# A gated linear attention followed by a mixer: three more transposes on the transfer queue, one product folded into another, and a new order

## The chip, the cores and the metric

The kernel runs on one core of a Trainium2 chip. The metric is the device time of one execution in microseconds (us), the lower the better. A core has five engines that each work through their own instruction list in order: PE (TensorE, matrix products; its weight loads are listed apart as PEld), DVE (VectorE), ACT (ScalarE), POOL (GpSimd) and SP (SyncE, which here issues every transfer). The transfers themselves run on 16 DMA engines. Products land in PSUM, in eight banks; everything else is worked on in SBUF.

## The reference

For 4 batches, 8 heads, 768 time steps and a head width of 48, a recurrent state is decayed, updated and read at each step; the result, as a 768 x 384 matrix `x` for each batch, goes through a low-rank mix over time and an MLP over the 384 columns.

```python
for t in range(S):
    state = alpha[:, :, t, :, None] * state + einsum('bhd,bhe->bhde', k[:, :, t], v[:, :, t])
    y[:, :, t] = einsum('bhd,bhde->bhe', q[:, :, t], state)
x = y.transpose(0, 2, 1, 3).reshape(B, S, H * D)
h = x.transpose(0, 2, 1) @ U @ V                 # U 768 x 32, V 32 x 768
u = x + h.transpose(0, 2, 1)
out = u + maximum(u @ w_ch1, 0) @ w_ch2          # 384 -> 1536 -> 384
```

## The kernel before

Each batch's 768 steps are cut into six chunks of 128 (`c` from 0 to 5). `b0` to `b3` below are the four batches, so the third batch is `b2`. A chunk loads four tiles of 192 KB (alpha, k, q, v) into the 40 `io` buffers. The chunks named by `PAIRS` (all of b0, four of b1) go through `stage_pair`, the others through `stage_gla`. `stage_gla` does this for a chunk:

- ACT takes the logarithm of alpha (`lt`, line 549); PE sums it over time (lines 556 and 558); ACT takes the exponentials `ai` and `aa` (566, 567).
- POOL or DVE multiplies k by `ai` and q by `aa` into one tile, `rkq` (577).
- k and q are transposed into `kqt`. In b2 and in the last two chunks of b1 PE does that: two groups of four 128 x 128 products (line 591) into two PSUM banks, and two copies out of PSUM (lines 290 on DVE, 288 on ACT, through the helper `copy`). In b3, by the tuple `QUEUE_T`, one `dma_start_transpose` on SP's queue does it (line 603), which reads and writes SBUF alone.
- PE forms the scores from `kqt` (619), DVE masks them into `pm` (629), PE forms the state's update from `rkq` and `rv` (642, not from `kqt`), DVE and POOL carry the state on (669, 653), and PE forms the chunk's output (681, 686), which ACT or DVE copies into `xb` (288, 290).

`stage_mix` forms the low-rank mix of a batch, `mlp1` the first MLP product (line 815, 24 groups of three products a batch, with a ReLU on ACT at 825 or on DVE at 827) and `mlp2` the second (line 841, 18 groups of four a batch, 21 in b3, with an addition on DVE at 847 and a store on SP at 850 or 852). In b1 to b3 the mix adds the V product to `xb` and stores `u` in `ub` (732, 742). In b0, by `SUM_U`, `u` transposed is summed in PSUM (752, 764) for `mlp1`, and `u` itself is formed besides: one V product for each chunk (line 755) into a bank of its own, and a DVE addition into `ub` (765), which `mlp2` adds to its product at 847. In b3 `u` is transposed by three transfers on SP's queue (770).

Nothing schedules at run time. `TABLE` lists all steps in one order with the engine that each goes to, and `SLOTS` the buffer each takes; every engine runs its own steps in that order and waits on semaphores for what they need. SP is one queue too: a transfer that waits for its operand holds back every transfer behind it. There are four `rkq` and four `kqt` buffers, and a transposing transfer waits until the last reader of its `kqt` buffer is through.

Of the kernel before, what the change touches and what calls it, by code (L numbers as in the profile page):

```python
# [11 lines left out]
ALU = mybir.AluOpType  # L12
# [17 lines left out]
F+DB+SJXPK2ALHAJhPJYDK1AK6GB9SJlPIyDKNAJTPKOAJmDK5GKgABySI-PK4AJiDKPAK3AJLPLiAKKGKQDBuSJPPJADJDPJQABxSJRPJUAKhAJBPLfABzS  # L30
JbPJCDKiALhAI3PKjAJEDLxAKlGCMSJVPJcAJMDJfPI4DJWAB3SKRGKZPKSPJgDLJPI7PKaDKkGLKAB6SJSDI9PLNALgAI8DK8PLjGCFSK7PK+AI+DJHPKeG
LMAK9DKmPCESOEAJjPLkDJIAKtPKnPLLACVSKuDI5PKoAKTPKvGJkAJNPB5SKVDKpAJZPI6DKzGKUAJdPB7SJaDJOAK-PJeAKqPKWPKrDLlPGHPCCSKXDLCP
GIPLADB-SLnDJFPLBDLzPCBSJ-PJGAKYDNhAJJPLIGLDDCGSNjPLPGKsDJtPNkACUSNlALEDKAPLOGL1ANoDNmAKbPCQSL0AKBPJKDL3GLdAKcDLQPNnALXP
CDSLFPLSAL2GLYDLmPLRPCLSLoALZDL5PJuPNpGLTAL7DKCDLsPKwPLGDGJPCYSKxALtDL4PCXSGKDJvPOWAL6DOYPLyGJwDCISLUPOZALuGL8PLWDLpPOoA
CKSJ5PObAL+DJnPL9DNqSOqPLrDJ6POsALVDJoPGeSLqDNyACWSLaPOrAJ7PCZSOcAOaAL-POuALbALvPCSSMADOtAJpPLwAJ8DN0PJqDMBPCHSNrPMCAN3A
MDPNsDCRSOwGJzPMEDKEPMGDOvGCNSMHDJ0PMFDNzGOxSMIPJ1PMKDNiAMLDMNPMMDO6ACJSKFPMJDN1AOdGCOSNtDMOANuPMRPJ2DMPPOeGN4AN2AKGPMQD
NwPMSDOfSO8PMZPO+AMlPMaDMXPCPSN6DMmAMVPO9ACTSN5DNxAM7PNvDMYAN-PN7SM5PMWDOADNBPM8DOGPKDSKHDOHAOgPOFGM9POpAGGSNCDM6AOLGMtP
OhDGYSOJAOIAM-PCaSM+AOBGMfPOMDGdSNAAM3PMgDOXGONSORPMTPOSDM1POiDMUAMrPCbSOKAM4DOTGMxPMsAM2DMnPMuAMyDPAGOjPMpPMoAOkDOmPO-G
N8POnDOyPMzPN9DPBSO7GMhPN+DMdPOzDGLSMjPO0DO1PJ9SMbPMkAOlDGMSMqAMvPMiAO2DNDPMcAMwAO3DO4PMeAPCPO5DOOPNcPPDDOPDNEPOQDOCPNFP
PEDOUPODDPFPOVDNIPPGANGDM0APHPNSPPIAPJPNdPPKDPNDNTPPLDPMDPOPNUPPRDPTSPPDNJPPSDPQDNePNVDPUSNNPNXPPVSNOPNYPKISNKPJySNZPNWS  # L40
NPPPYPPWPPZDPaPPXDPyPNLDPbAP6PNQDNMSPePP7ANRSPwPPfDJrSP0PGXSP8PP1APqPPkPPrDQCPPlAPuPPzAQDDPgPNaDP+PPvDPhAP4PPxAP9APmPP5D
PsPP-DPiPNfDPcPPtDNgSQEPPjDPdAJ3SQfPF-SQAPJ+SP2PQBDGFSQQPPnDP3AJsSQkPJ4SPoPNHSQRPGSSPpDQGPQFDNbSGRSQlPJxSQHPQLPQmPQMPQnD
QIPQoSQSPGASQJDQNPQTDQKSQgPQODQUSQVPQPSQhPQWPQiDQaPQXPQjSQbPQYDQcPQZSQdDQeS
"""
SLOTS = """
ABCDEFAGAHAIAAJBBCKCALADBMENBAOFBPBCGBCHAQCAACEGRAHDSCTAEBBFGUAABDDVCHAWFECDABBXCDAYCBGCECZFBCCCaAAEDbFDGcACEABBAdAGBACF
HDBCACCeEHECDfBBBACgGEhBBAHADiCBCCGEjDBFCkHBAlmBGDAEAnDAHFBAACAGCAADBACAHDDFFBGECBCHAHAGICDEFCBKAGCECADHBBALFHJBBMADOAGB
CBBAEFQAPDNDGSBCHFBRDGACUCBTAEBVCDWHADBBAECGHBDAZBFEBHAAGXDFAHYAEBBaDAbdCeHfgFGDDCFGEDBhEGCFiAEcCCDljkFnBAmEADCBBBCFAEDC
CDFFCAADBGEBCGHEACBDBACKHBAABJBBHCAAICEQDABAPCDAABNBFOECHAACLBACFDREADDGSCABFAVBECDDHUDBBGWADFECHABGTCFBZBCAXBBDEAaCBHBM
BBCADFYACCCEAbDDBCFdCEAeACfAEghAFAcjBDCDCACGEBkHBBDCAAAAmCBCCEABiBGGFJCAACEBHDCDBFCCIBDEHDBDHBQADKCDBPEBHAAGAFAENCBBEAGA  # L50
FBABHDOCEBEFAAGBDCCWBHACCEFACHLDEFCDBBAHCGEFAADDACHCGCEAHDBDCGEABCBDGEUCBBDGHFACDFGASHFCGBDBRCZGDEHCGECGTBEFGCXDHEBAGCDB
AabYMFjDm
"""


# [98 lines left out]
def mm(*cols):  # L154
    return sum(max(c / 2.4 + 2.5, 25.0) for c in cols)
# [3 lines left out]
def kernel(  # L159
# [178 lines left out]
    def paired(b, c):  # L338
        return c // 2 < PAIRS[b]
# [22 lines left out]
    def xk(b, xb, c):  # L362
        return [(xb, c, 0), (xb, c, 1)] if paired(b, c) else [(xb, c)]
# [331 lines left out]
    def stage_mix(b, xb, ub, uT):  # L695
# [63 lines left out]
                    P.add({"PE": mm(TW)}, lambda e, j=j, f=f_h: f(e, j), r=[utx, ("ve", tt)], w=[tb[j]])  # L759
                    P.add({"ACT": 390, "DVE": 470}, lambda e, j=j, tt=tt, tb=tb: copy(e, uT()[:, j, tt * TW : (tt + 1) * TW], tb[j]()[:, 0:TW]), r=[tb[j]], w=[(uT, tt, j)])  # L760
        for c in range(NC):
            hb = Buf(bank) if b in SUM_U else None
            if b in SUM_U:
                P.add({"PE": mm(DM)}, lambda e, c=c, hb=hb: nc.tensor.matmul(hb()[:, 0:DM], lhsT=(ve_sb if paired(b, c) else vm_sb)[:, c * C : (c + 1) * C], rhs=utx(), start=True, stop=True), r=[utx, ("ve" if paired(b, c) else "vm", c // NT)], w=[hb])
                P.add({"DVE": 465}, lambda e, c=c, hb=hb: nc.vector.tensor_tensor(ub()[:, c, :], xb()[:, c, :], hb()[:, 0:DM], op=ALU.add), r=[hb] + xk(b, xb, c), w=[(ub, c)])
            if b in QUEUE_U:
                if c % 2 == 1:
                    P.add(
# [7 lines left out]
            elif c % 2 == 1 and b not in SUM_U:  # L776
                ub2 = Buf(bank)

                def f_tr(e, c=c, ub2=ub2):
                    t = bf(ub2()).rearrange("p (e c) -> p e c", c=C)  # L780
                    n = 0
                    for cc in (c - 1, c):
                        for j in range(NCT):
                            nc.tensor.matmul(t[:, n, :], lhsT=ub()[:, cc, j * C : (j + 1) * C], rhs=ident, start=True, stop=True, is_transpose=True)  # L784
                            n += 1

                P.add({"PE": mm(*[C] * 6)}, f_tr, r=quarters(ub, (c - 1, c)), w=[ub2])
# [6 lines left out]
                P.add({"DVE": 450, "ACT": 710}, f_ev, r=[ub2], w=[(uT, c // 2)])  # L794

    def u_half(uT, ct, tt, by_chunk):
        if not by_chunk:
# [30 lines left out]

            P.add({"ACT": 395, "DVE": 470}, g, r=[hb], w=[(h1, tt, jt)])

    def mlp2(b, ub, h1, c):
        tt = c // NT
        ou = Buf(io)
        parts = [(0, DM)] if (b, c) != (B - 1, LAST) else [(0, CUT), (CUT, DM)]
        for n, (lo, hi) in enumerate(parts):
            hb = Buf(bank)
            for g in range(3):

                def f(e, g=g, hb=hb, lo=lo, hi=hi):
                    for jt in range(4 * g, 4 * g + 4):  # L840
                        nc.tensor.matmul(  # L841
                            hb()[:, 0 : hi - lo], lhsT=h1()[:, jt, c * C : (c + 1) * C], rhs=w2_sb[:, jt, lo:hi],
                            start=(jt == 0), stop=(jt == NJ - 1),
                        )

                P.add({"PE": mm(*[hi - lo] * 4)}, f, r=[(h1, tt, jt) for jt in range(4 * g, 4 * g + 4)] + [("w2", jt) for jt in range(4 * g, 4 * g + 4)], w=[hb])
            P.add({"DVE": 468}, lambda e, hb=hb, lo=lo, hi=hi: nc.vector.tensor_tensor(flat(ou)[:, lo:hi], ub()[:, c, lo:hi], hb()[:, 0 : hi - lo], op=ALU.add), r=[hb] + ([(ub, c)] if b in SUM_U else quarters(ub, (c,))), w=[(ou, n)])  # L847
# [11 lines left out]
    for b in range(B):  # L859
# [3 lines left out]
        for c in range(NC):  # L863
# [3 lines left out]
            else:  # L867
                x = stage_gla(b, c, whole, xb)
                whole = [(x, 0, x)]
        stage_mix(b, xb, ub, uT)  # L870
        mlp1(b, uT, h1, 0)
        mlp1(b, uT, h1, 1)
        for c in range(NC):
            mlp2(b, ub, h1, c)
    P.run("".join(TABLE.split()), "".join(SLOTS.split()))


# [28 lines left out]
```

## Time and profile before

| | us |
|---|---|
| runs shown: median (lowest to highest of 3) | 160.37 (159.43 to 160.62) |
| the profiled execution | 159.65 |
| its span, first to last instruction | 157.9 |

The span leaves 1.75 us around it. In the page of the profile a busy share is the time in which an engine had an instruction in it. PE's products are pipelined, so that share says when PE had nothing, not how fast it ran; the granted clock is 1.00 throughout. The chain of waits goes back from the last instruction and names at each step what released it. In the timeline a row gives start, duration, engine, line, output and inputs, and a count of like instructions.

### The profile page before, as it was taken

The page shows a single profiled execution, that of the slowest core. Times are in us where ns is not written, and L with a number is a line of the kernel's source. Part 1 is how long each engine was busy: PE and PEld are TensorE (multiplying, and loading weights), DVE is VectorE, ACT ScalarE, POOL GpSimd, SP SyncE. Part 2 cuts the span into 40 slices and gives each one's busy share as a digit, 9 for nine tenths or more (in the row PEclk, how much of TensorE's full clock was granted, in tenths as well). Part 3 has the DMA queues.
Part 4 walks back from the last instruction along what each step waited for, and adds up shares of the span by engine and source line. Part 5 has one row for each costly group of instructions (what it writes and reads, how often), then busy time and mean ns, then how long its engine had stood idle before and what let it go on. Part 6 is the DMA issues. An engine that isn't in the chain of part 4 may idle for free.

```text
span 157.9 us, 4730 instructions
## 1 busy us (share of the span) xinstructions
PE 147.7 (94%) x1836; PEld 98.7 (63%) x1836; DVE 118.6 (75%) x264; ACT 83.6 (53%) x219; POOL 58.6 (37%) x93
## 2 busy tenths in 40 slices
PE   0499999999999999999999999999999999999992
PEld 0268777766665665767668676766667556665662
DVE  5048998999899788869799978989999714484252
ACT  3667899775866823988838464457362001441000
POOL 8336787387838300446358223416610000000000
PEclk9999999999999999999999999999999999999999
DMA  5999999999999999999799998996860073406662
GB/s 130 280 312 309 257 263 253 337 317 274 279 254 236 269 177 200 201 216 209 156 210 222 179 200 176 201 153 152 174 143 3 15 142 124 150 34 159 185 224 100
DMA packets 96966, 31.08 MB, mean 197 GB/s; under 512 B 90640, under 2 KB 96912, under 8 KB 96944
## 3 DMA queue, kind: packets, MB, share of 16 engines
q1 hardware_dynamic: 96944, 30.78, 82.0%
q8 instruction: 14, 0.23, 0.6%
q14 instruction: 8, 0.07, 0.1%
HBM read 23.89 MB, written 4.72 MB: 181 GB/s over the span
## 4 chain that ended last, share of the span: by engine, by line
PE 72%; SPq 14%; DMA 5%; DVE 3%; issue 2%; ACT 1%
PE ps L815 29%; PE ps L841 28%; SPq L347 11%; DMA io<-in_alpha_dram 5%; PE ps L619 2%; PE ps L686 1%; PE ps L556 1%; PE ps L591 1%; PE ps L784 1%; PE ps L681 1%; DVE rkq L577 1%; SPq L295 1%; SPq L320 1%; PE ps L642 1%; PE ps L732 1%
## 5 line engine op out<-in xcount | busy, mean ns | idle before, releaser
L841 PE MATMUL ps<-w_sb,h1t 128*128 128x384 bf16 (+2 forms) x300 | 52.8, 320 | 0.0
L815 PE MATMUL ps<-uT,w_sb 128*128 128x384 bf16 x288 | 52.0, 326 | 0.0
L825 ACT ACTIVATE h1t<-ps 128x384 bf16<-128x384 f32 x50 | 23.1, 499 | 28.8 <-PE ps L815 28.7
L815 PEld LDWEIGHTS <-w_sb 128*128 128x128 bf16 x288 | 26.6, 98 | 16.0
L841 PEld LDWEIGHTS <-h1t 128*128 128x128 bf16 x300 | 26.8, 97 | 15.0
L827 DVE TENSOR_SCALAR h1t<-ps 128x384 bf16<-128x384 f32 x46 | 24.1, 552 | 12.9 <-PE ps L815 12.2
L629 DVE TENSOR_TENSOR pm<-ps,maskc 128x512 bf16<-128x512 f32 x28 | 17.7, 681 | 1.8 <-PE ps L619 1.3
L847 DVE TENSOR_TENSOR io<-ub,ps 128x384 f32<-128x384 bf16 (+2 forms) x25 | 13.1, 532 | 6.1 <-PE ps L841 5.8
L577 POOL TENSOR_TENSOR rkq<-io,aa 128x384 bf16<-128x384 f32 x9 | 8.2, 915 | 19.6 <-PE ps L815 10.3
L461 DVE TENSOR_TENSOR pm<-ps,maskp 128x512 bf16<-128x512 f32 x20 | 13.3, 686 | 1.6 <-PE ps L450 1.2
L292 POOL CAST rv<-io 128x384 bf16<-128x384 f32 x17 | 9.5, 557 | 11.6 <-DMA io<-in_v_dram 6.7
L577 POOL TENSOR_TENSOR rkq<-io,ai 128x384 bf16<-128x384 f32 x11 | 10.0, 916 | 6.0 <-DMA io<-in_k_dram 4.7
L288 ACT CAST xb<-ps 128x192 bf16<-128x192 f32 (+1 forms) x20 | 7.2, 374 | 9.0 <-PE ps L686 7.0
L742 DVE TENSOR_TENSOR ub<-xb,ps 128x288 bf16<-128x288 bf16 x24 | 9.3, 449 | 2.7 <-PE ps L732 2.5
L290 DVE COPY kqt<-ps 128x512 bf16<-128x512 bf16 x21 | 8.7, 418 | 2.3 <-PE ps L426 1.8
L292 POOL CAST w_sb<-io 128x384 bf16<-128x384 f32 x14 | 8.2, 587 | 4.1 <-DMA io<-in_moe_w_ch_dram 4.0
L288 ACT COPY kqt<-ps 128x512 bf16<-128x512 bf16 x15 | 8.7, 597 | 1.7 <-PE ps L426 0.7
L566 ACT ACTIVATE ai<-ps 128x384 bf16<-128x384 f32 x14 | 6.9, 495 | 3.5 <-PE ps L558 2.9
L549 ACT ACTIVATE lt<-io 128x384 bf16<-128x384 f32 x14 | 7.1, 524 | 2.8 <-issue 2.8
L567 ACT ACTIVATE aa<-ps 128x384 bf16<-128x384 f32 x14 | 6.8, 495 | 3.3 <-PE ps L558 1.7
L408 POOL TENSOR_TENSOR rkq<-io,aa 128x384 bf16<-128x384 f32 x8 | 7.2, 910 | 3.4 <-ACT aa L401 3.2
L426 PE MATMUL ps<-ident,rkq 128*128 128x128 bf16 x80 | 8.3, 236 | 0.1
(117 smaller groups left out, 222.8 us busy)
## 6 DMA issues: line engine op xcount, KB each, us to landing
io<-in_alpha_dram SPq DMA_DIRECT2D x24, 192.0 KB, 3.8
io<-in_v_dram SPq DMA_DIRECT2D x24, 192.0 KB, 3.9
io<-in_k_dram SPq DMA_DIRECT2D x24, 192.0 KB, 4.1
io<-in_q_dram SPq DMA_DIRECT2D x24, 192.0 KB, 3.8
io<-in_moe_w_ch_dram SPq DMA_DIRECT2D x24, 192.0 KB, 4.2
out_dram<-io SPq DMA_DIRECT2D x13, 192.0 KB, 1.9
out_dram<-io SPq DMA_DIRECT2D x20, 96.0 KB, 2.2
out_dram<-io SPq DMA_DIRECT2D x1, 120.0 KB, 1.7
```

The costliest lines, as they stand in the source:

```text
L288: nc.scalar.copy(dst, src)
L292: nc.gpsimd.tensor_copy(dst, src)
L347: lambda e: nc.sync.dma_start(t().rearrange("p (h j) d -> p h (j d)", j=2), src[b, hs, sl, :].rearrange("h (p j) d -> p h (j d)", j=2)),
L461: nc.vector.tensor_tensor(dst, s2, maskp.to_broadcast([C, 2, 2, C]), op=ALU.mult)
L577: eng.tensor_tensor(dst()[:, :, 0:D], a(), x(), op=ALU.mult)
L629: nc.vector.tensor_tensor(pm()[:, :, par, :], s2, maskc.to_broadcast([C, HP, C]), op=ALU.mult)
L742: nc.vector.tensor_tensor(v(ub), v(xb), qb[g]()[:, 0 : NT * W].rearrange("p (c d) -> p c d", c=NT), op=ALU.add)
L815: nc.tensor.matmul(hb()[:, 0:TW], lhsT=w1_sb[:, ct, jt * 128 : (jt + 1) * 128], rhs=u_half(uT, ct, tt, b in QUEUE_U), start=(ct == 0), sto ...
L825: nc.scalar.activation(dst, hb()[:, 0:TW], AF.Relu)
L827: nc.vector.tensor_scalar_max(dst, hb()[:, 0:TW], 0.0)
L841: nc.tensor.matmul(hb()[:, 0 : hi - lo], lhsT=h1()[:, jt, c * C : (c + 1) * C], rhs=w2_sb[:, jt, lo:hi], start=(jt == 0), stop=(jt == NJ - 1),
L847: P.add({"DVE": 468}, lambda e, hb=hb, lo=lo, hi=hi: nc.vector.tensor_tensor(flat(ou)[:, lo:hi], ub()[:, c, lo:hi], hb()[:, 0 : hi - lo], ...
```

## The change

1. `QUEUE_T` also holds chunks 3, 4 and 5 of b2. Their k and q are transposed by three transfers on SP's queue in place of 24 PE products and six copies out of PSUM.
2. b0's V product is the first product of the `mlp2` group in its own PSUM bank, with `start` set there and no longer on the first of the twelve. The six additions into `ub` (765) are gone, b0 uses no `ub`, and the addition at 847 takes `xb` in place of `ub`. The number of products stays the same. `utx` and `xb` of b0 are held until its `mlp2` is through.
3. `TABLE` and `SLOTS` are new: every engine's order, which engine does a step that two could do, and the buffers. The table is one line shorter, so line numbers of the changed kernel are lower by one up to `stage_mix`.

```diff
 TABLE = """
-BASA8SBDSABSBISBESA9SCcAA+SCePA-SC0GBJSAFGCfAChABQSDjAAJPCzABBSDlPCgABCSCiDC1PDnABKSCjDCkPBYSCdGCmABMSAGPDmABGSC4AC3AClP
+BESDKAA+SBASCzAA8SCcACePC1PBISDMPDjABBSCfACgACjGA-SC4AA9SBDSBCSC2AC5DBJSCdGC3AC6GBKSDlPDoAC0GC7PChAC9ADmAClPCnACiDCkPCmA
...
-    QUEUE_T = tuple((3, c) for c in range(6))
+    QUEUE_T = tuple((3, c) for c in range(6)) + ((2, 3), (2, 4), (2, 5))
...
         for c in range(NC):
-            hb = Buf(bank) if b in SUM_U else None
-            if b in SUM_U:
-                P.add({"PE": mm(DM)}, lambda e, c=c, hb=hb: nc.tensor.matmul(hb()[:, 0:DM], lhsT=(ve_sb if paired(b, c) else vm_sb)[:, c * C : (c + 1) * C], rhs=utx(), start=True, stop=True), r=[utx, ("ve" if paired(b, c) else "vm", c // NT)], w=[hb])
-                P.add({"DVE": 465}, lambda e, c=c, hb=hb: nc.vector.tensor_tensor(ub()[:, c, :], xb()[:, c, :], hb()[:, 0:DM], op=ALU.add), r=[hb] + xk(b, xb, c), w=[(ub, c)])
...
-    def mlp2(b, ub, h1, c):
+    def mlp2(b, xb, utx, ub, h1, c):
+        low = b in SUM_U
...
                 def f(e, g=g, hb=hb, lo=lo, hi=hi):
+                    if low and g == 0:
+                        nc.tensor.matmul(hb()[:, lo:hi], lhsT=ve_sb[:, c * C : (c + 1) * C], rhs=utx()[:, lo:hi], start=True, stop=False)
                     for jt in range(4 * g, 4 * g + 4):
                         nc.tensor.matmul(
                             hb()[:, 0 : hi - lo], lhsT=h1()[:, jt, c * C : (c + 1) * C], rhs=w2_sb[:, jt, lo:hi],
-                            start=(jt == 0), stop=(jt == NJ - 1),
+                            start=(jt == 0 and not low), stop=(jt == NJ - 1),
                         )
...
-            P.add({"DVE": 468}, lambda e, hb=hb, lo=lo, hi=hi: nc.vector.tensor_tensor(flat(ou)[:, lo:hi], ub()[:, c, lo:hi], hb()[:, 0 : hi - lo], op=ALU.add), r=[hb] + ([(ub, c)] if b in SUM_U else quarters(ub, (c,))), w=[(ou, n)])
+            P.add({"DVE": 468}, lambda e, hb=hb, lo=lo, hi=hi: nc.vector.tensor_tensor(flat(ou)[:, lo:hi], (xb if low else ub)()[:, c, lo:hi], hb()[:, 0 : hi - lo], op=ALU.add), r=[hb] + (xk(b, xb, c) if low else quarters(ub, (c,))), w=[(ou, n)])
```

The order moves at three places on SP that the prediction speaks of. First the start of the queue, which feeds b0. Before, the first rows are:

```order
L347 DMA io0_134<-in_alpha_dram 128x4x96
L347 DMA io1_135<-in_alpha_dram 128x4x96
L347 DMA io2_136<-in_v_dram 128x4x96
L296 DMA v_in_65<-in_moe_V_dram 32x768
L347 DMA io3_137<-in_alpha_dram 128x4x96
L347 DMA io4_138<-in_alpha_dram 128x4x96
L347 DMA io5_139<-in_k_dram 128x4x96
```

Now they are:

```order
L346 DMA io0_134<-in_alpha_dram 128x4x96
L346 DMA io1_135<-in_q_dram 128x4x96
L346 DMA io2_136<-in_alpha_dram 128x4x96
L346 DMA io3_137<-in_alpha_dram 128x4x96
L346 DMA io4_138<-in_alpha_dram 128x4x96
L346 DMA io5_139<-in_k_dram 128x4x96
L346 DMA io6_140<-in_v_dram 128x4x96
```

The alpha of b0's chunk 0, with which PE begins in both orders, was the second transfer and is the fourth; the load of V (`v_in`) has gone back to the 28th place. The last of b0's 24 loads was the 28th transfer and is the 26th.

Second, the place where the three new transposes stand, among the loads of b2 and b3. Before, the same stretch of the queue holds loads alone:

```order
L354 DMA io23_157<-in_k_dram 128x8x48
L354 DMA io26_160<-in_q_dram 128x8x48
L354 DMA io12_146<-in_alpha_dram 128x8x48
L354 DMA io24_158<-in_alpha_dram 128x8x48
L354 DMA io27_161<-in_v_dram 128x8x48
L354 DMA io29_163<-in_v_dram 128x8x48
```

Now it holds (`kqt1`, `kqt2` and `kqt3` are those of b2's chunks 3, 4 and 5):

```order
L353 DMA io26_160<-in_q_dram 128x8x48
L602 DMA_TRANSPOSE kqt1_190<-rkq0_80 128x8x128
L353 DMA io25_159<-in_v_dram 128x8x48
L353 DMA io28_162<-in_alpha_dram 128x8x48
L602 DMA_TRANSPOSE kqt2_191<-rkq3_83 128x8x128
L602 DMA_TRANSPOSE kqt3_192<-rkq2_82 128x8x128
L353 DMA io19_153<-in_v_dram 128x8x48
```

Behind the first of them 21 loads of b2 and b3 are still queued.

Third, the end of the transposes, with the last loads of b3. Before:

```order
L603 DMA_TRANSPOSE kqt1_190<-rkq2_82 128x8x128
L852 DMA out_0_dram<-io30_164 128x384
L850 DMA out_0_dram<-io37_171 64x384
L850 DMA out_0_dram<-io0_134 64x384
L354 DMA io22_156<-in_q_dram 128x8x48
L850 DMA out_0_dram<-io39_173 64x384
L603 DMA_TRANSPOSE kqt2_191<-rkq0_80 128x8x128
L354 DMA io11_145<-in_v_dram 128x8x48
L603 DMA_TRANSPOSE kqt0_189<-rkq2_82 128x8x128
```

Now (`kqt0` is that of b3's chunk 5, the last `kqt1` that of its chunk 4):

```order
L602 DMA_TRANSPOSE kqt2_191<-rkq3_83 128x8x128
L353 DMA io16_150<-in_k_dram 128x8x48
L353 DMA io7_141<-in_v_dram 128x8x48
L353 DMA io22_156<-in_v_dram 128x8x48
L849 DMA out_0_dram<-io5_139 64x384
L602 DMA_TRANSPOSE kqt0_189<-rkq2_82 128x8x128
L602 DMA_TRANSPOSE kqt1_190<-rkq1_81 128x8x128
```

Ahead of the last transpose stood, since the first load of b2, 48 loads, five transposes and five stores (four of 96 KB and one of 192 KB); now 48 loads, eight transposes and one store of 96 KB stand there.

More of the change, by code (lines that the diff above doesn't have):

```diff
@@ L53 @@
+BFCCBCHAECHBAABACIBDABCDBJKNPACCABCOBBDGFLBHEADGEQAADFGDRBCBHSCEAFGDABADCBBHFDBDMWVEBCGAACEFABACBXEYAABCCGCBUaBFHDZABGBE
+bcHAAFGBCHCBCDABAGAFdCATBfelDCCCBCDBHCEDFAHDkjABCCDDnEABAACAAHCDFBEBCHDFCBCmHEDDBCGPBGCBCHBOANDAEKCFBCBDCHSBEDEBFBCCBHEB
+AAGDBCBALCHGDAEHDGBCFDCCEBQHGBHFWACBEBADCADGHCABABCDGDRHDCBGBAFHDCBDAFAHAYUVFBBDEGHFEXDHMEBHGACHFACHFGEDFADBZcTlEjHf
 """
@@ L794, in stage_mix @@
                 P.add({"DVE": 450, "ACT": 710}, f_ev, r=[ub2], w=[(uT, c // 2)])
+        return utx
     def u_half(uT, ct, tt, by_chunk):
@@ L842, in f @@
                             hb()[:, 0 : hi - lo], lhsT=h1()[:, jt, c * C : (c + 1) * C], rhs=w2_sb[:, jt, lo:hi],
[L843 removed]
+                            start=(jt == 0 and not low), stop=(jt == NJ - 1),
                         )
[L846 to L847 removed]
+                P.add({"PE": mm(*[hi - lo] * 4)}, f, r=[(h1, tt, jt) for jt in range(4 * g, 4 * g + 4)] + [("w2", jt) for jt in range(4 * g, 4 * g + 4)] + ([utx, ("ve", tt)] if low and g == 0 else []), w=[hb])
+            P.add({"DVE": 468}, lambda e, hb=hb, lo=lo, hi=hi: nc.vector.tensor_tensor(flat(ou)[:, lo:hi], (xb if low else ub)()[:, c, lo:hi], hb()[:, 0 : hi - lo], op=ALU.add), r=[hb] + (xk(b, xb, c) if low else quarters(ub, (c,))), w=[(ou, n)])
             if paired(b, c):
@@ L869 @@
                 whole = [(x, 0, x)]
-        stage_mix(b, xb, ub, uT)
+        utx = stage_mix(b, xb, ub, uT)
         mlp1(b, uT, h1, 0)
@@ L873 @@
         for c in range(NC):
-            mlp2(b, ub, h1, c)
+            mlp2(b, xb, utx, ub, h1, c)
     P.run("".join(TABLE.split()), "".join(SLOTS.split()))
```

62 lines of the change are left out of this document (29 added, 33 removed).

## The prediction

> **What bounds the kernel now.** I read the page's busy shares and slices first, then a table of busy time by stages, then the chain of waits.
>
> ```profile
> span 157.9 us, 4730 instructions
> PE 147.7 (94%) x1836; PEld 98.7 (63%) x1836; DVE 118.6 (75%) x264; ACT 83.6 (53%) x219; POOL 58.6 (37%) x93
> DMA  5999999999999999999799998996860073406662
> ```
>
> PE leads, but a busy share averages over unlike stages; the transfers are near full for three quarters of the span. The table, with columns window, length, busy time (and count) of each engine, granted clock, share of the DMA engines and GB/s, separates them:
>
> ```profile
> 14.30:31.40 17.10, 16.44 (x355) 12.68 (x354) 15.84 (x36) 15.38 (x46) 10.28 (x16) 1.00 1.02 279
> 31.40:55.00 23.60, 23.45 (x319) 14.86 (x318) 21.45 (x48) 16.94 (x45) 15.33 (x26) 1.00 1.03 273
> 55.00:88.00 33.00, 33.00 (x391) 22.38 (x390) 28.25 (x59) 21.72 (x58) 13.38 (x18) 1.00 1.00 197
> 88.00:117.00 29.00, 28.79 (x347) 19.18 (x346) 25.86 (x53) 15.38 (x42) 10.96 (x14) 1.00 0.90 174
> 117.00:124.90 7.90, 7.90 (x143) 5.10 (x140) 6.40 (x13) 1.97 (x6) 0.00 (x0) 1.00 0.12 30
> 124.90:155.00 30.10, 30.10 (x204) 18.73 (x196) 14.23 (x29) 4.58 (x10) 0.00 (x0) 1.00 0.47 136
> ```
>
> Until 31.4 the recurrence of b0 runs while loads arrive, and DVE (15.84 of 17.10), ACT and the transfers are all nearly full. From 31.4 to 155 PE is without work for only 0.15 + 0.21 us in the rows shown. From 55 to 88 the DMA share is 1.00 as well.
>
> ```profile
> PE 72%; SPq 14%; DMA 5%; DVE 3%; issue 2%; ACT 1%
> 31.57 1.00 PE ps L815 x6
> 71.95 0.22 PE ps L591 x4
> 131.57 10.24 PE ps L815 x63
> 145.22 9.79 PE ps L841 x72
> 155.03 0.30 DVE io L847
> ```
>
> The chain (start, duration, what) goes through SP's loads, then PE from the first MLP product at 31.57 to 155. So a microsecond of PE work removed after 31 shortens the span by one, as long as PE's next operand is there. The transfers could undo that.
>
> **The change part by part.** The sum is made against the profiled execution, 159.65 us (span 157.9 and 1.75 around it); that is 0.72 below the median 160.37 of the runs shown, so the result is carried over to the median.
>
> *Transposes on PE.* Six groups of four leave. A group takes 0.22 us on the chain (above), so 6 x 0.22 = 1.3 us. All six lie in the stages 55 to 88 and 88 to 117, where PE had no gap to swallow them: -1.3 us on the path.
>
> ```profile
> L290 DVE COPY kqt<-ps 128x512 bf16<-128x512 bf16 x21 | 8.7, 418 | 2.3 <-PE ps L426 1.8 <-PE ps L591 0.4
> L288 ACT COPY kqt<-ps 128x512 bf16<-128x512 bf16 x15 | 8.7, 597 | 1.7 <-PE ps L426 0.7 <-PE ps L591 0.5 <-DVE pm L461 0.3
> L765 DVE TENSOR_TENSOR ub<-xb,ps x6: 545/545/555, 29.0 to 34.5; 128x384 bf16<-128x384 bf16 x6
> ```
>
> *Copies and additions.* By the order DVE does five copies fewer and ACT one: 5 x 0.418 = 2.1 and 0.6 us; the six additions are 6 x 0.545 = 3.3 us of DVE. Both run beside PE. PE's idle time of 0.36 us after 31.4 is all that they can give back there, so I count 0, with -0.4 as the far end. If that cover were absent, DVE being the bound, they would give 5.4.
>
> *The V product.* Six products stay, in another bank: 0 on PE. The new wait, the first group of four for `utx`, ends long before: `utx` serves the first MLP product at 31.57, and the first group of four comes after some 17 us more of PE work in the new order, counted at the durations of the rows. Holding `xb` and `utx` of b0 costs nothing as long as b0's last group is done (after 52 us of PE work) before b2 needs that `utx` (after 80).
>
> *SP and the DMA engines.* Three transposes come in.
>
> ```profile
> L603 SPq DMA_TRANSPOSE kqt<-rkq x6: 1232/1412/2187, 88.4 to 113.9; - x6
> DMA to landing us min/median/max: 3.1/3.4/3.5
> 126.00:127.00 1.00, 1.00 (x8) 0.59 (x6) 1.00 (x3) 0.00 (x0) 0.00 (x0) 1.00 0.93 183
> 131.00:132.00 1.00, 1.00 (x8) 0.60 (x7) 0.00 (x0) 0.00 (x0) 0.00 (x0) 1.00 0.87 281
> ```
>
> Each takes 1.41 us of SP, 4.2 in all. At 126 only transposes are moving, at 183 GB/s and a share of 0.93; 262,144 bytes (128 x 1024 of two bytes) then take 1.43 us of all DMA engines, 4.3 for three. In exchange four stores (491,520 bytes, 1.7 us at the 281 GB/s of the stores at 131) go behind the last transpose: net +2.6 us of transfers ahead of it. The Trainium skill, "DMA: Bandwidth & Descriptors", section "Latency and other measured facts", gives 261 GB/s for a transposing DMA; by that three would take 3.0 and the net be +1.3. The trace's 183 decides.
>
> Does that reach PE? These rows show the end of the loads before:
>
> ```profile
> 111.64 0.57 SPq L354 DMA_DIRECT2D io<-in_v_dram  x1
> 113.91 1.24 SPq L603 DMA_TRANSPOSE kqt<-rkq  x1
> 117.51 0.62 PE L619 MATMUL ps<-kqt 48*128 48x128 bf16 x16
> SPq L603 <- PE ps L619: 2.0, 1, 2.0
> SPq L603 <- POOL rkq L577: 1.9, 2, 1.3
> ```
>
> The last transpose was issued at 113.91, landed 3.4 later at 117.3, and its scores began at 117.51: 0.2 us of slack. But SP had stood idle for 1.7 us just before it (112.21 to 113.91); the last two rows (us in total, times, longest) put its stands at transposes down to PE and POOL, not to the transfers. In the new order the three transposes of b2 have eight and more us of PE work (counted from the order at the rows' durations) between the release of their `kqt` buffer and their scores. The tightest, b3's chunk 4, can be issued once the output of chunk 3 has read its buffer, and from there PE has two scores (0.26 each), four groups of three (0.49), two of four (0.65), two updates (0.17), one output (0.37) and chunk 5's scores (0.26), 4.8 us, against 3.4 until landing. Its bounds are 0 and the +2.6 us with PE waiting for all but 0.2 less 0.9 (PE comes to it sooner), so 0 to 3.3. I take 0, since the order leaves 1.4 us and SP's idle time can take up the rest.
>
> *The start.*
>
> ```profile
> 17.64 1.05 SPq L347 DMA_DIRECT2D io<-in_v_dram  x2
> 3.96 0.52 ACT L377 ACTIVATE lt<-io 128x384 bf16<-128x384 f32 x1 [1.94 <-DMA io<-in_alpha_dram]
> 4.54 0.48 PE L386 MATMUL ps<-lt,upto 128*128 128x384 bf16 x1 [4.54 <-ACT lt L377]
> 4.81 0.36 PE L387 MATMUL ps<-lt,below 128*128 128x192 bf16 x1
> 7.13 0.47 PE L308 MATMUL ps<-v_bf,sel 32*128 32x384 bf16 x1 [1.68 <-POOL v_bf L302]
> 14.72 0.33 PE L386 MATMUL ps<-lt,upto 128*128 128x384 bf16 x1
> 14.88 0.25 PE L387 MATMUL ps<-lt,below 128*128 128x192 bf16 x1
> ```
>
> An issue takes about 0.53 us (1.05 for two, b0's last loads). PE's first operand is two places later, 1.1 us later to begin; b0's last load is two places earlier, 1.1 us earlier to end. Which counts depends on whether DVE and ACT, both full from 14.3 on, are the limit. I take 0, with -1.1 and +1.1 as ends. The tail is unchanged: in both orders ten groups of four stand between b3's last mix product and its first MLP product.
>
> Sum: -1.3 + 0 + 0 + 0 + 0 = -1.3. The execution of 159.65 becomes 158.3, the median 160.37 becomes **159.0 us**.
>
> **The rivals.**
>
> *The queue holds (slower).* A transpose waiting on SP holds b3's loads, the last transposes land late, and PE stands at the scores of chunk 5 or 4. For it: the 0.2 us of slack, 2.6 us more transfers, a DMA share of 1.00. Against it: SP's idle time and the 4.8 us. It decides once that last transpose lands more than 1.4 us later than the order allows; at its far end PE waits 3.3, giving 160.37 - 1.3 + 3.3 = 162.4.
>
> *The start gains (faster).* b0's loads end 1.1 us sooner, DVE has 5.4 us less to do, and PE's small waits go: 160.37 - 1.3 - 1.1 - 0.4 = 157.6. For it: DVE's 93% until 31.4. Against it: the additions left out ran from 29.0 on, at the end of that stage.
>
> *PE runs slowly for longer.* From 4.54 to 4.81 a product of 384 columns took 270 ns, from 14.72 to 14.88 it took 160, at a granted clock of 1.00. If the later first product delays that switch by 1.1 us, up to 41% (110 of 270) of it is lost, 0.5 us; if by the 2.6 us between the first product and the second burst at 7.1, which the start's ends cover too, 1.1: 160.1 at most. Against it, PE is not the limit then.
> The Trainium skill, "TensorE: Matmul & The Clock Gate", Part 1, puts the switch to full rate after a busy window of about 3.4 us; one window more would cost 1.4 us by these rows, and the trace shows the two rates, but its full rate only some time between 7.1 and 14.7.
>
> *Nothing comes of it.* PE's 1.3 us return as waits for 3.4 us landings, 160.4; this is the first rival at mid-range and is counted there.
>
> **How the numbers follow.** Chances: forecast 0.42, queue 0.25, start 0.22, slow PE 0.11. One per cent, 1.6 us, is about what a measurement can tell from no change, and the forecast's 1.3 lies just inside. With runs that scatter by 1.2 us I give the forecast 0.15 to faster, 0.26 to same, 0.01 to slower; the start's case 0.19 and 0.03; the queue's 0.06 to same, 0.19 to slower; the slow PE 0.06 and 0.05. Together 0.34 faster, 0.41 same, 0.25 slower. The range takes the start's 157.6 and the queue's 162.4, each widened by 0.9, the way from the median to the lowest run: 156.7 to 163.3.
>
> **What would show it.** Right: line 602 nine times, line 590 with 40 products, PE without a gap from 55 to 155, the first MLP product at about 30.4 (its V products no longer come first), and b3's first one near 130. Wrong: PE idle before line 618 with SP as releaser, an SP stretch standing on a transpose while the DMA share falls below 1.0 between 75 and 105, or a first MLP product after 32.

## The result, and the profile after

| | before | after |
|---|---|---|
| median, us (lowest to highest of 4) | 160.5 (159.43 to 160.68) | 162.19 (161.79 to 162.53) |
| ratio after to before (95% interval) | | 1.0138 (1.0096 to 1.0180) |
| the profiled execution, us | 159.65 | 162.18 |
| its span, us | 157.9 | 160.4 |

The change made the kernel 1.4% slower. The page of the changed kernel, the lines that answer to those of before:

```profile
span 160.4 us, 4662 instructions
PE 146.3 (91%) x1812; PEld 97.5 (61%) x1812; DVE 111.2 (69%) x247; ACT 84.8 (53%) x221; POOL 60.2 (38%) x96
DMA  5999999999997899999997998999990096057493
```

PE has its 24 products fewer and DVE 7 us less to do; the span is 2.5 us longer. The table of stages (window, length, busy time and count of PE, PEld, DVE, ACT, POOL, granted clock, DMA share, GB/s) says where PE went idle:

```profile
31.40:55.00 23.60, 22.26 (x304) 14.52 (x303) 19.03 (x42) 15.02 (x40) 14.84 (x24) 1.00 0.97 257
55.00:88.00 33.00, 32.85 (x374) 21.67 (x374) 26.00 (x54) 23.00 (x64) 12.95 (x17) 1.00 1.00 196
88.00:117.00 29.00, 27.65 (x341) 18.12 (x336) 24.09 (x48) 14.64 (x37) 11.37 (x15) 1.00 1.04 187
117.00:124.90 7.90, 7.36 (x124) 5.09 (x123) 6.29 (x12) 3.84 (x9) 1.27 (x2) 1.00 0.37 66
124.90:155.00 30.10, 30.10 (x209) 17.97 (x208) 12.56 (x27) 6.11 (x14) 0.00 (x0) 1.00 0.53 138
```

PE's idle time after 31.4 was 0.36 us in all; now it is 1.34, 0.15, 1.35 and 0.54. The DMA share from 88 to 117 rose from 0.90 to 1.04. PE's waits of the changed kernel (total, times, longest, in us):

```profile
PE ps L555 <- DVE io L846: 1.3, 1, 1.3
PE ps L555 <- ACT lt L548: 0.9, 1, 0.9
PE ps L618 <- DMA kqt<-rkq: 0.5, 1, 0.5
PE ps L590 <- POOL rkq L576: 0.5, 1, 0.5
```

Two of the four are the sum over time of a `stage_gla` chunk (line 555, was 556), which needs only that chunk's alpha.

To compare kernels I use one more figure, PE's lost time: over PE's timeline, the time from one row's start to the next, less the row's products at their closest spacing (162.7 ns for 384 columns, 55 ns for a transpose, and so on by line). It counts idle time and slow products alike. Before: 139.7 us of dense work and 15.6 us lost until 75, 1.6 after. Changed: 138.3 dense, 16.9 lost until 75, 3.9 after. So 1.3 us of work went, 1.3 us of loss came before 75 and 2.3 after it.

The experiments ran on other chips in five sets, each beside the kernel before, where executions scattered more (the kernel before from 159.2 to 165.3 us). Executions over 1.5% above the fastest of their kernel are left out of the ratios, and no reading of lost time rests on the profiles of e2, e9, e14, e15 and e17, which were of such executions.

### The profile page after: what moved, and what is told of

It reads as the page before. It is cut to its first block, busy times and chain, and to the rows that moved or that the text cites. A ratio compares the mean times of both kernels' runs of the same rounds, so it can differ in the third digit from the quotient of the medians.

```text
span 160.4 us, 4662 instructions
## 1 busy us (share of the span) xinstructions
PE 146.3 (91%) x1812; PEld 97.5 (61%) x1812; DVE 111.2 (69%) x247; ACT 84.8 (53%) x221; POOL 60.2 (38%) x96
## 4 chain that ended last, share of the span: by engine, by line
PE 68%; DMA 11%; SPq 11%; DVE 2%; POOL 2%; ACT 2%; issue 2%; POOLq 0%; DVEq 0%
PE ps L840 26%; PE ps L811 25%; SPq L346 10%; DMA io<-in_q_dram 6%; DMA io<-in_k_dram 3%; PE ps L618 2%; DMA kqt<-rkq 2%; POOL rkq L407 1%; PE ps L685 1%; PE ps L555 1%; PE ps L779 1%; PE ps L590 1%; PE ps L680 1%; DVE ub L741 1%; PE ps L731 1%
## 5 line engine op out<-in xcount | busy, mean ns | idle before, releaser
L840 PE MATMUL ps<-w_sb,h1t 128*128 128x384 bf16 (+2 forms) x300 | 53.5, 320 | 0.0
L821 ACT ACTIVATE h1t<-ps 128x384 bf16<-128x384 f32 x56 | 25.9, 497 | 27.9 <-PE ps L811 27.6
L840 PEld LDWEIGHTS <-h1t 128*128 128x128 bf16 x300 | 27.0, 98 | 15.5
L823 DVE TENSOR_SCALAR h1t<-ps 128x384 bf16<-128x384 f32 x40 | 20.9, 551 | 7.6 <-PE ps L811 7.2
L846 DVE TENSOR_TENSOR io<-ub,ps 128x384 f32<-128x384 bf16 (+2 forms) x19 | 9.8, 529 | 15.3 <-PE ps L840 15.1
L287 ACT CAST xb<-ps 128x192 bf16<-128x192 f32 (+1 forms) x23 | 8.3, 393 | 13.2 <-PE ps L685 7.8
L291 POOL CAST rv<-io 128x384 bf16<-128x384 f32 x20 | 10.2, 520 | 10.7 <-DMA io<-in_v_dram 10.7
L576 POOL TENSOR_TENSOR rkq<-io,aa 128x384 bf16<-128x384 f32 x8 | 7.6, 951 | 14.1 <-PE ps L731 6.8
L407 POOL TENSOR_TENSOR rkq<-io,aa 128x384 bf16<-128x384 f32 x10 | 9.4, 941 | 6.9 <-DMA io<-in_q_dram 5.9
L385 PE MATMUL ps<-lt,upto 128*128 128x384 bf16 x10 | 4.1, 410 | 6.7 <-ACT lt L376 6.7
L291 POOL CAST w_sb<-io 128x384 bf16<-128x384 f32 x13 | 6.6, 515 | 7.7 <-DMA io<-in_moe_w_ch_dram 7.7
L652 POOL TENSOR_TENSOR st<-sm,tot 128x384 bf16<-128x384 f32 x6 | 5.3, 883 | 7.3 <-ACT xb L287 3.8
```

Of the source, the lines that this page charges most:

```text
L287: nc.scalar.copy(dst, src)
L291: nc.gpsimd.tensor_copy(dst, src)
L407: eng.tensor_tensor(jh(dst()[:, :, 0:D]), raw(a), jh(x()), op=ALU.mult)
L576: eng.tensor_tensor(dst()[:, :, 0:D], a(), x(), op=ALU.mult)
L821: nc.scalar.activation(dst, hb()[:, 0:TW], AF.Relu)
L823: nc.vector.tensor_scalar_max(dst, hb()[:, 0:TW], 0.0)
```

## The experiments

### What each part does in the old order

Each part of the change was put into the order of before. For the V product only the six products' own steps and the six additions leave that order; against the changed kernel, the code differs by this line, beside `TABLE` and `SLOTS`:

```diff
-    QUEUE_T = tuple((3, c) for c in range(6)) + ((2, 3), (2, 4), (2, 5))
+    QUEUE_T = tuple((3, c) for c in range(6))
```

> The kernel before with its own order, where only the first batch's V product is moved into the bank of the second MLP product (six matmuls and six additions on VectorE fall out of the order, nothing else moves). The prediction took 0 for this part. If that holds: 0.996 to 1.003 of the kernel before. Rival: the fold makes PE wait, since the addition of x must now follow the second product and reads another tile: slower by up to 0.5%. Other rival: VectorE's 2.8 us of additions stood in the way of PE's operands: faster by 0.3 to 0.6%. If it is 0, the loss of the changed kernel lies in the new order and the transposes.

Measured: 1.0123 (1.0027 to 1.0219). A second and a third time, and the kernel before as one of a set:

> The V product's move alone in the old order, a second time with more runs beside it. Taken as 0: ratio 0.997 to 1.004. If it costs (six additions less on VectorE, but the last additions read another tile and PE's product is started by another operand): 1.005 to 1.010, which would be a third or more of the changed kernel's loss.

> The V product's move alone in the old order, a third time. If it costs what the second run gave: 1.004 to 1.010, and 3 us of PE's lost time after 88 us, as in its two profiles (3.03 and 3.05). If it is free, as the prediction took it: 0.997 to 1.004, and lost time after 88 us as in the kernel before.

> The kernel before, unchanged: a ratio of 1.000 within 0.4 points if the comparison has no bias; PE's lost time after 88 us 1.5 to 2.0 us, as in its two profiles.

> The kernel before once more, unchanged, for a second profile of it beside the others of this set. Both theories: a ratio of 1.00; its PE lost (starts less dense work) is 17.2 us in the first profile, and how far it lies from that here says how much of a difference of two profiles is the kernel's.

Measured: e15 1.0070 (1.0013 to 1.0127), e18 1.0055 (1.0013 to 1.0098); the kernel before against itself 0.9985 (0.9914 to 1.0055) in e5 and 1.0019 (0.9967 to 1.0071) in e17. In e18 PE loses 1.6 us after 75, as much as in the first profile of before, though e4 lost 3.8. No wait is common to these profiles that before lacks. So moving the V product gained nothing. All three intervals lie above 1, with middles from 0.55 to 1.2%, so it seems to cost something; the kernel before against itself is off by up to 0.2%, and no profile shows where such a cost would lie.

For the transposes, three transfers go into SP's queue of before, each where its operands are ready, and the scores of b2's chunk 5 stand 2 us further back on PE:

```diff
 L354 DMA io_160<-in_q_dram 128x8x48
+L603 DMA_TRANSPOSE kqt_190<-rkq_83 128x8x128
 L354 DMA io_146<-in_alpha_dram 128x8x48
 L354 DMA io_158<-in_alpha_dram 128x8x48
+L603 DMA_TRANSPOSE kqt_192<-rkq_81 128x8x128
 L354 DMA io_161<-in_v_dram 128x8x48
 L354 DMA io_163<-in_v_dram 128x8x48
 L354 DMA io_165<-in_alpha_dram 128x8x48
 L354 DMA io_166<-in_v_dram 128x8x48
+L603 DMA_TRANSPOSE kqt_189<-rkq_82 128x8x128
 L354 DMA io_169<-in_alpha_dram 128x8x48
```

> The kernel before with its own order, where only k and q of the third batch's chunks 3 to 5 are transposed by SyncE's transfers: 24 transposes (1.3 us of PE) and 6 copies fall out, three transfers are put where their operands are ready (one each ahead of three loads), and the scores of chunk 5 with what hangs on them stand 2 us further back on PE. Theory 'transfers' (the queues are full until the last loads, so 4 us more of transfers make loads late): PE idles 1.3 to 3 us more between 88 and 125 us, the time is 1.000 to 1.010 of the kernel before. Theory 'new order' (the loss comes from where the new order puts loads): PE's 1.3 us are gained, 0.990 to 0.994.

> The change without its new order: the kernel before with both the V product folded into the second MLP product and the three transposes on SyncE's queue, put as in the run with the transposes alone. Theory 'new order': 0.988 to 0.994 of the kernel before, since both parts are free in the old order. Theory 'transfers': as with the transposes alone, 1.000 to 1.010. Rival 'fold' (moving the V product makes PE wait): 0.3 to 1.0 points above the run with the transposes alone.

Measured: 1.0306 (1.0176 to 1.0436) with the transposes alone, 1.0295 (1.0208 to 1.0383) with both parts. This is the largest effect of any part of the change, and above what either theory expected: 24 products fewer on PE, and some 4.9 us more. PE's longest wait after its start in e6:

```profile
PE ps L556 <- ACT lt L549: 2.9, 1, 2.9
```

The windows around it, columns as above:

```profile
84.00:88.00 4.00, 3.46 (x53) 2.36 (x52) 3.97 (x7) 1.72 (x6) 4.00 (x5) 1.00 1.04 181
88.00:92.00 4.00, 1.32 (x9) 0.68 (x7) 2.16 (x5) 0.87 (x2) 0.61 (x1) 0.98 1.23 147
92.00:96.00 4.00, 3.82 (x29) 2.21 (x29) 2.48 (x4) 1.19 (x4) 1.29 (x2) 0.50 1.30 224
96.00:100.00 4.00, 4.00 (x37) 2.15 (x36) 0.50 (x1) 1.70 (x5) 0.00 (x0) 0.66 1.05 207
```

SP's rows in the timeline of e6 (start, duration of the issue) and ACT's logarithm show the cause:

```profile
83.83 1.85 SPq L603 DMA_TRANSPOSE kqt<-rkq  x1
85.74 1.19 SPq L354 DMA_DIRECT2D io<-in_alpha_dram  x2
87.11 2.08 SPq L603 DMA_TRANSPOSE kqt<-rkq  x1
...
93.38 1.89 SPq L603 DMA_TRANSPOSE kqt<-rkq  x1
...
91.61 0.52 ACT L549 ACTIVATE lt<-io 128x384 bf16<-128x384 f32 x1 [3.08 <-DMA io<-in_alpha_dram]
```

No gap over 0.2 us lies ahead of a transpose: SP waited for nothing. Yet each held the queue for about 1.9 us, 5.8 in all, and the alpha loads behind them came late. The logarithm waited 3.1 us for alpha, and PE for the logarithm, 2.9 us. That alpha was issued at 86.42 and landed 5.2 us later; in e5, the kernel before again, the same load was issued at 83.64 and landed after 3.8. So it was late by its issue and by its transfer. Then the granted clock fell to 0.50 and 0.66 for 4 us each, although PE was busy there: 4 x 0.50 + 4 x 0.34 = 3.4 us more. In e6 PE loses 9.0 us after 75 and in e7 8.2, against 1.6 in the first profile of before and 3.0 in e5's.

### Whether it is the issue or the transfers

> The kernel before, with two more plain loads of 192 KB, which nobody reads, in each of the three places where the run with the transposes in the old order has a transfer: six loads, 1.15 MB, at 200 GB/s 5.8 us of the queue; PE's work is that of the kernel before. Theory 'transfers on a full queue': the loads behind them come 4 to 6 us later, PE waits some 3 to 5 us between 85 and 105 us, ratio 1.02 to 1.035. Theory 'issue' or something in the transposes alone: six loads are issued in 0.6 us each, 3.5 us, ratio under 1.02.

The edit: six `io` buffers are loaded with parts of k that nobody reads, two in each place where e6 has a transpose; the kernel before is otherwise untouched.

```diff
+    for i in range(6):
+        x = Buf(io)
+        P.add({"SP": 700.0}, lambda e, x=x, i=i: nc.sync.dma_start(x(), k[2, :, i * C : (i + 1) * C, :].rearrange("h t d -> t h d")), w=[x])
     P.run("".join(TABLE.split()), "".join(SLOTS.split()))
```

Measured: 1.0374 (1.0281 to 1.0466). Plain loads of 1.15 MB cost as much as the three transposes (6.0 us, against 4.9 and the 1.3 that e6 saves on PE), with PE's work unchanged, a little above the range of the theory 'transfers'. Their rows in the timeline of e14:

```profile
84.18 1.87 SPq L877 DMA_DIRECT2D io<-in_k_dram  x2
88.11 3.23 SPq L877 DMA_DIRECT2D io<-in_k_dram  x2
94.92 1.67 SPq L877 DMA_DIRECT2D io<-in_k_dram  x2
```

A load's issue takes about 0.57 us where it isn't drawn out (in before at 111.64); here two take 1.7 to 3.2, 6.8 us for six. So an issue can be drawn out in this stretch. A full share alone doesn't say when: in the changed kernel two loads were issued in 0.58 and 0.57 us (at 89.52 and 90.14) with a share of 1.20 from 88 to 92. What the six loads show is that plain transfers here are paid as transposes are. The other way to tell issue and transfer apart is another engine that issues:

```diff
-                {"SP": 900.0},
-                lambda e: nc.sync.dma_start_transpose(
+                {"SP": 900.0, "ACT": 900.0},
+                lambda e: (nc.sync if e == "SP" else nc.scalar).dma_start_transpose(
```

> As the run with the transposes alone in the old order (1.031 of the kernel before), but the three transfers are issued from ScalarE's queue, when ScalarE has little to do; SyncE's queue has the loads alone, in the old order. Theory 'issue' (SyncE is held 1.9 us by each, so loads are late): the waits of 2.9 us for alpha near 88 us are gone and PE's 1.3 us are gained, ratio 0.992 to 1.003. Theory 'transfers' (the DMA engines are full, whoever issues): alpha stays late, ratio 1.015 to 1.03.

> The changed kernel, where the third batch's three transfers are issued from ScalarE's queue at about the time at which SyncE issues them. Theory 'issue': SyncE reaches alpha of the fourth batch's chunk 2 some 5 us earlier, PE's idle near 99 us is gone, 0.8 to 1.5 us below the changed kernel, ratio 1.002 to 1.007. Theory 'transfers': within 0.5 us of the changed kernel, 1.010 to 1.018.

Measured: 1.0364 (1.0301 to 1.0427) and 1.0388 (1.0325 to 1.0452), both by the numbers a case for the transfers. The rows of e13 say otherwise: ACT was itself held.

```profile
81.23 1.92 SPq L354 DMA_DIRECT2D io<-in_alpha_dram  x2
81.31 3.53 ACTq L603 DMA_TRANSPOSE kqt<-rkq  x1
84.90 0.52 ACT L549 ACTIVATE lt<-io 128x384 bf16<-128x384 f32 x1 [3.44 <-DMA io<-in_q_dram]
85.47 0.32 PE L556 MATMUL ps<-lt,ut_ones 128*128 128x384 bf16 x1 [3.24 <-ACT lt L549]
```

Alpha was issued early, at 81.23, but one of the three transposes took 3.53 us of ACT's queue (the other two about 1.25 each), and the logarithm stood behind it. In e16 PE waited 4.7 us for the transposes themselves (line 618), which landed later. These two show that a transpose can hold ACT as it holds SP; they don't part the transposes' issue from their transfer. Nor does e14, whose loads held SP too. It shows that nothing peculiar to a transpose is needed.

### What the new order does

> The changed kernel's order, with the third batch's chunks 3 to 5 transposed on PE again (24 more transposes on PE, 6 more copies, no such transfers on SyncE's queue): only this part of the change undone. Dense PE work rises by 1.3 us. Theory 'transposes' (they hold SyncE from 84.2 to 89.5 us, 1.9 us of waiting and 3.4 of issue, and so make the alpha load behind them late): SyncE reaches that alpha load about 4 us earlier, the PE idle of 1.31 us near 99 us is gone, 1.3 us paid and 1.3 to 1.9 won: time within 0.5 us of the changed kernel or 0.5 below it. Theory 'late loads' by the order alone (the queue is short of transfers' time, not of issue): the load is hardly earlier, the idle stays above 0.8 us, and the time is 0.8 to 1.3 us above the changed kernel, at about 1.020.

> The changed kernel's order with the third batch's transposes on PE again, a second time, beside the changed kernel on the same chip. Theory 'transfers' as the two runs in the old order gave it (three transfers cost some 6 us of waits there): if they cost as much in the new order, this is 3 to 4 us faster than the changed kernel. If the new order was made so that PE has other work while they run, they cost there about what they save: within 0.8 us of the changed kernel, and what remains of the loss is the new order's own.

> The changed kernel once more, unchanged, as the measure for the other three of this set, on one chip. Both theories: 1.010 to 1.018 of the kernel before, as it was; a second profile shows which of its four waits (38.6, 50.3, 98.7, 119.2 us) come again.

The edit is the diff shown first above, with the new order; the 24 products stand a little ahead of their scores. Measured: e3 1.0169 (1.0074 to 1.0265), e10 1.0107 (1.0059 to 1.0156), the changed kernel beside e10 1.0134 (1.0053 to 1.0215). The stages from 88 of e10:

```profile
88.00:117.00 29.00, 28.74 (x363) 19.08 (x362) 24.15 (x49) 16.43 (x42) 11.18 (x16) 1.00 0.91 165
117.00:124.90 7.90, 7.90 (x128) 5.52 (x126) 7.01 (x14) 4.07 (x9) 1.28 (x2) 1.00 0.32 62
```

Without the three transfers PE's idle time after 88 goes from 1.89 to 0.26 us, and the DMA share of the stage from 1.04 to 0.91. Lost time after 75 is 2.5 us in e3 and 2.6 in e10, against 3.9 in the changed kernel: the transposes cost 1.3 to 1.4 us of lost time there and save 1.3. Two profiles of one kernel can differ by as much (before 1.6, e5 3.0), but the other profiles of the new order part the same way, with 4.2 in e8 and 3.8 in e11, which have the three transfers, and under 3 in e12, which has not. The ratios agree as far as they reach: e9 and e10, on one chip, can't be told apart. In the old order the transposes cost three to six times what they save (9.0 and 8.2 us in e6 and e7, less the 1.6 to 3.8 of before, e5, e4 and e18), so the new order does take most of their price away. But it costs something itself, since without the three transfers it is still 1.1 to 1.7% slower than before, of which the V product's move may be a part: until 75 PE loses 16.9 us in the changed kernel, 18.0 in e3 and 17.1 in e10, against 15.6, 16.3, 16.3 and 16.7 in before, e5, e4 and e18.

### Whether single late loads are to blame

> The changed kernel, with one load moved three places up in SyncE's queue: alpha of the second batch's chunk 4, for which ScalarE's logarithm waited 1.34 us and behind it PE near 38.6 us. Theory 'late loads' (two alpha loads that the new order issues late cost most of what was lost): the PE idle before that cumulative sum falls from 0.9-1.0 us to under 0.3, and the time falls by 0.6 to 1.0 us below the changed kernel's, that is to about 1.007-1.010 of the kernel before. Theory 'transposes' (the third batch's three transposes on SyncE's queue cost the time): no change, 1.013, since that stall lies before the first transpose. A third outcome, that PE's wait moves to the next operand (the w1 and w2 loads that are now half a microsecond later): idle gone at 38.6 but back before 45, no change in time.

> The changed kernel with two loads exchanged in SyncE's queue: alpha of the fourth batch's chunk 2 goes up to the place of v of its chunk 3, five places earlier, and v goes down to alpha's place. At 98.7-100.8 us PE idles 1.31 us before that chunk's cumulative sum; the profile names VectorE's last addition (100.23-100.78) as the releaser, and ScalarE's logarithm ended at the same time (100.75) after 2.69 us of waiting for this alpha. Theory 'late loads': the logarithm starts some 3 us earlier, the idle is gone or under 0.4 us, and the time falls by 0.9 to 1.3 us, to about 1.005-1.008 of the kernel before. Rival 'bank' (PE waits for VectorE, whose eight additions of 3.12 us stand before the one named): the logarithm is early, the idle of 1.3 us stays, the time stays at 1.013.

> The changed kernel with both alpha loads earlier in SyncE's queue (the second batch's chunk 4 three places up, the fourth batch's chunk 2 exchanged with v of chunk 3). Theory 'late loads': both idles gone (0.9 and 1.3 us), time 1.5 to 2.2 us below the changed kernel, 1.000 to 1.005 of the kernel before. Theory 'transfers': the waits move to the loads and transposes that come behind, PE's lost time between 88 and 125 us stays above 2.5 us, and the time stays at 1.010 to 1.016.

> The new order with the transposes on PE and alpha of the second batch's chunk 4 three places up in SyncE's queue. If the new order's own loss is that late load (0.9 to 1.4 us of idle near 39 us in three profiles): 0.8 to 1.2 us below the same kernel without the move. If the wait only moves on to other loads: the same within 0.4 us.

The edits, in SP's rows, e1 and then e2; e8 has both, and e12 has the first with the transposes on PE:

```diff
+L353 DMA io_143<-in_alpha_dram 128x8x48
 L346 DMA io_139<-in_k_dram 128x4x96
 L319 DMA io_140<-in_moe_w_ch_dram 128x384
 L319 DMA io_141<-in_moe_w_ch_dram 128x384
-L353 DMA io_143<-in_alpha_dram 128x8x48
...
-L353 DMA io_164<-in_v_dram 128x8x48
+L353 DMA io_136<-in_alpha_dram 128x8x48
 L353 DMA io_171<-in_v_dram 128x8x48
...
-L353 DMA io_136<-in_alpha_dram 128x8x48
+L353 DMA io_164<-in_v_dram 128x8x48
```

Measured: e1 1.0147 (1.0018 to 1.0276), e2 1.0120 (0.9920 to 1.0319), e8 1.0167 (1.0033 to 1.0301), e12 1.0096 (1.0062 to 1.0130) against e10's 1.0107. The idles did go, near 39 us in e1, e8 and e12 and near 99 us in e8. In the changed kernel, PE and what ended beside its wait near 99 us:

```profile
100.81 0.32 PE L555 MATMUL ps<-lt,ut_ones 128*128 128x384 bf16 x1 [1.31 <-DVE io L846]
100.23 0.52 ACT L548 ACTIVATE lt<-io 128x384 bf16<-128x384 f32 x1 [2.69 <-DMA io<-in_alpha_dram]
100.23 0.55 DVE L846 TENSOR_TENSOR io<-ub,ps 128x384 f32<-128x384 bf16 x1
```

And the same place in e8:

```profile
101.02 0.52 ACT L548 ACTIVATE lt<-io 128x384 bf16<-128x384 f32 x1
102.92 0.33 PE L555 MATMUL ps<-lt,ut_ones 128*128 128x384 bf16 x1
103.83 0.55 DVE L846 TENSOR_TENSOR io<-ub,ps 128x384 f32<-128x384 bf16 x1
```

In e8 alpha was in time, and PE went on 0.9 us before the addition at 846 even began. So the addition that the profile names released nothing; the two ended within 0.03 us of each other, and alpha was the cause. That settles the wait and not the time: e8 still loses 4.2 us after 75, a part of it at other operands (the transposed `u` near 106, a later alpha, the last transposes), and the time stayed. Expected were 1.000 to 1.005. Loads in a full queue that are moved up move others down.

> The changed kernel, where the transfers for the third batch's chunks 4 and 5 stand two loads further back in SyncE's queue, so that SyncE issues two loads in the 1.9 us (84.2 to 86.1) in which it stands waiting for VectorE's and GpSimd's scaling. Theory 'standing' (the cost of a transfer is SyncE's wait in front of it): DMA share in 84-88 us rises from 0.79 to about 1.0, alpha of the fourth batch's chunk 2 is issued 1 to 2 us earlier, PE's idle near 99 us falls from 1.31 to under 0.5, time 0.5 to 1.2 us below the changed kernel. Theory 'transfers' (the 1.4 us of issue and the transfer itself): the idle stays above 0.9 and the time within 0.4 us. The transposes land later too: up to 1 us more at the scores near 91.5 us is possible and would be seen as a wait there.

The edit puts two of SP's transposes two loads further back. Measured: 1.0243 (1.0161 to 1.0326), where 0.5 to 1.2 us less than the changed kernel was expected. A window of the changed kernel and the same one of e11:

```profile
84.00:88.00 4.00, 3.89 (x34) 2.20 (x33) 4.00 (x8) 1.82 (x6) 3.92 (x5) 1.00 0.79 157
84.00:88.00 4.00, 3.90 (x46) 2.57 (x43) 3.96 (x7) 2.28 (x9) 3.68 (x4) 1.00 1.23 198
```

And PE's wait there:

```profile
PE ps L618 <- DMA kqt<-rkq: 1.8, 2, 1.4
```

SP no longer stood (DMA share 1.23 for 0.79), and the idle near 99 was gone, but the transposes landed late: PE waited 1.4 us for them near 92. The lost time after 75 is 3.8, as with the changed kernel. The wait changed places once more. The profile is of e11's fastest execution (163.58 us, median 165.69), so it doesn't show why the others were slower still.

## Why the prediction was wrong

The forecast was 1.3 us faster than before; measured were 1.7 us slower. The gain was there and was paid back, and the new kernel lost more besides.

- *Transposes on PE, -1.3.* Right in size: dense work fell from 139.7 to 138.3 us.
- *SP and the DMA engines, 0 with ends 0 and 3.3.* This is the step that failed. "I take 0, since the order leaves 1.4 us and SP's idle time can take up the rest" weighed the last transposes alone, where in fact PE waited only 0.5 us, and asked nothing of the 21 loads queued behind the first new transpose. In the old order the three transfers cost PE 4 to 7 us more lost time; in the new order 1.3 to 1.4, which is all that they save. The estimate of 4.3 us of transfers was not contradicted, and the row with a share of 1.00 from 55 to 88 said that little would hide them. One of the prediction's signs of being wrong came too: SP stood before a transpose from 84.2 to 86.1, in the window with a share of 0.79. But e11 removed that stand and gained nothing.
- *The premise.* "So a microsecond of PE work removed after 31 shortens the span by one, as long as PE's next operand is there": the reservation decided. PE was full and the DMA engines were full beside it; work taken from one and given to the other gained nothing.
- *Copies and additions, and the V product, each 0.* Nothing was gained, so 0 was right for the copies and additions as far as the runs tell. The V product's 0 is in doubt: alone it measures 1.0055 to 1.0123, some 0.9 to 2.0 us, with no wait that would explain it.
- *The start, 0 with ends -1.1 and +1.1.* PE's first product came 2.2 us later (6.71 for 4.54), not 1.1, and the first MLP product even so at 30.22, as the prediction's sign has it. In the first pair of profiles 0 is right: 13.9 us lost until 31.4 before, 14.0 after. Over all profiles that may be read so, seven in the old order lose 13.9 to 15.2 (mean 14.7) and eight in the new one 14.0 to 17.6 (mean 15.5). The difference of 0.8 lies within the stated ends and comes for the most part from e8 and e11, with waits of 1.6 and 1.4 us for POOL's `rkq` of a paired chunk near 25 us.
- *The new order itself.* Beside the start the sum held no term for it before 75. From 31.4 to 75 the changed kernel lost 2.9 us against 1.7, and the new order without the transposes measures 1.0107 and 1.0169, of which the V product may be a part. e1, e8 and e12 show that it isn't the one late alpha load. What in the order costs it stays open, and with it the cause of about as much as was lost in the end.
- *The rival.* "The queue holds (slower)" gave 162.4 at its far end, and 162.2 was measured. That is luck for the most part. A load of b3 did come late behind a standing transfer (near 99 us), but PE waited 0.5 us at the last scores where the rival has 3.3, and e3 and e10 are about as slow without any of the three transfers.
- *PE runs slowly for longer.* It did, by the measure of the prediction's own rows. In the changed kernel:

```profile
14.68 0.53 PE L385 MATMUL ps<-lt,upto 128*128 128x384 bf16 x1
15.00 0.37 PE L386 MATMUL ps<-lt,below 128*128 128x192 bf16 x1
```

A product of 384 columns still took 320 ns at 14.68, where before took 160 at 14.72. The windows' granted clock reads 1.00 there in both kernels, as it does over the 270 ns products at the start, so this figure can't tell. No cost of it can be seen (13.9 and 14.0 us lost until 31.4), and the switch moves between executions of one order: in e5, the kernel before again, a product took 320 ns at 15.13.

## What to carry to other kernels

Where PE and the DMA engines are both full over the same stretch, moving work from one to the other trades, and here it traded at no gain at best; price it at the queue's own rate (here about 1.9 us of queue for a transpose of 256 KB against 0.44 us of PE for its two groups), and look at every load behind the new transfer, not at the transfer's own reader. A single late load in a full queue was here a symptom: moving it up made its wait vanish and left the time as it was. When a profile names a releaser that ended together with another candidate, a run that moves one of them tells which it was.

## What was not expected of the hardware

The granted clock fell after PE's waits in the middle of the kernel. After 2.9 us in e6 it was 0.50 and 0.66, as shown. After 1.9 us in e7, in windows of 2 us:

```profile
88.00:90.00 2.00, 0.53 (x10) 0.37 (x11) 0.29 (x1) 0.59 (x2) 0.00 (x0) 1.00 0.66 134
90.00:92.00 2.00, 2.00 (x21) 1.13 (x18) 1.62 (x3) 0.99 (x3) 0.89 (x2) 0.52 1.15 230
92.00:94.00 2.00, 2.00 (x13) 1.05 (x12) 0.86 (x2) 0.20 (x1) 0.40 (x1) 0.63 1.13 227
```

And in e8, after its 1.6 us wait near 25 us, where PE had gaps before and after:

```profile
26.00:28.00 2.00, 0.97 (x32) 0.89 (x34) 0.42 (x1) 0.00 (x0) 1.93 (x3) 0.88 0.86 235
28.00:30.00 2.00, 2.00 (x42) 0.88 (x36) 1.53 (x4) 1.91 (x6) 0.40 (x2) 0.50 1.07 298
30.00:32.00 2.00, 2.00 (x22) 1.65 (x17) 1.55 (x3) 1.24 (x4) 1.13 (x3) 0.50 1.08 340
```

The slow stretch comes behind the wait, and in e6 and e7 costs about as much again (3.4 us after 2.9, 1.7 after 1.9); in a busy share it can't be seen, since PE is busy there. It did not follow the 1.3 us wait of the changed kernel, nor one of 1.6 us in e1. The Trainium skill, "TensorE: Matmul & The Clock Gate", Part 1, has the clock go to half after an idle window of about 3.4 us; here shorter waits were enough at times, and the runs don't show where the limit lies.

A transpose's issue took 1.23 us of SP at the least and 1.85 to 2.08 in e6 among the loads; on ACT's queue one took 3.53.
